# Two-level seven-product scheme for the first MLP layer of batches 2 and 3, with its left-hand sums made in batch 1 and the Fourier front woven into the second layer before it

## The chip, the core and the metric

The kernel runs on one core of a Trainium2 chip. The metric is the device time of one launch in microseconds, the median of several runs. All arithmetic that matters here is fp32.

## What is computed

Four batches go through bucketed (hash) attention. Its output is rearranged to `x` of 768 rows by 512 columns per batch and put through a Fourier mixing, a normalisation and a two-layer MLP:

```python
X = np.fft.fft(x, axis=1); X = np.fft.fft(X, axis=2)
u = x + np.real(X)
un = (u - mean(u)) / sqrt(var(u) + 1e-6)      # per row
out = u + np.maximum(un @ w_ch1, 0) @ w_ch2   # 512 -> 2048 -> 512
```

## The kernel before

**Stages.** Attention for all batches comes first, with an order written out by hand, and ends at about 337 us; what this text is about lies behind it. There each batch `b` goes through `mix(b)`: the Fourier front (`cs` matmuls L1071, `A` and `B` matmuls L1100, DVE adds L1114), then `mlp7(b)`: first layer and second layer. The output of the first layer is held transposed, features by rows of the sequence, in `hall`. Batch 0 also builds the weights' block sums; the times of the later batches are 508.5 to 674.8, 674.8 to 841.9 and 841.9 to 1012.8 us.

**First layer.** One level of the Strassen-Winograd scheme: a 2 by 2 block product with seven products instead of eight. The left blocks are pieces of `w_ch1` (names `A11, A12, A22` for the plain ones, `S1` to `S4` for sums), made once in batch 0 by `quarters` (L1184) and stored to the DRAM tensor `ad` (L1196, L1197), 128 KB each. From batch 1 on, a ring of 12 slots takes them back from `ad` (L1357, on the SP queue); the trace calls these loads `w<-ad`. The right blocks are halves of `x` and four sums of them. A `product` (L1373) is two matmul instructions of 128x128 by 128x384 (L1384). For one block row `f`, `inner` (L1409) makes seven products; some accumulate on each other in PSUM (`px` holds the running sum, `p2` and `p5` two others). ACT copies `px` and `p5` to `hall` (L1424, L1431, L1434), DVE adds a bank to it (L1427, L1437, L1440), ACT applies relu (L1398, L1447). Eight block rows in two halves of four give 56 products a batch.

**Second layer.** `outer7(half)` (L1253) follows each half: again one level of the scheme, 7 products per row tile `j` of 256 columns (L1279), with sums of `hall` on DVE (L1263 to L1265), DVE adds of the results (L1291) and ACT copies (L1305). Its right blocks `w<-bd` (7 of 512 KB, L1284) are fetched again on SP's queue at the end of each `outer7`. So a batch is `inner(0)`, `outer7(0)`, `inner(1)`, `outer7(1)`; in batch 1 they stand at about 530, 566, 602.4 and 638.5 us.

**What else runs beside.** `across` (L1121) turns `u` back by PE transposes into a bank `un` and copies it out on ACT (L1127). `fold(b + 1)` (DVE, L971 on) prepares the next batch's front, stepped in `outer7(0)`. `guard` (L1471) reads all of q and k again (384 KB a load on POOL's queue, `nq`, three buffers, L1481) and squares them on ACT (L1492); its result decides in batch 3 whether a fallback is taken. `store` (L939) writes the output on POOL's queue for batches 0 to 2.

**What sets the order.** Each engine, and each DMA queue with the engine that issues into it, works its instructions strictly in order. In this part a scheduler orders the instructions by need, except where `in_turn()` (L693) ties an instruction behind the last one that was noted in `done_by`. Generators are stepped beside each other: a function yields, and what is stepped at the yield gets its place there. `pt` hands out one of the eight PSUM banks.

Of the kernel before, what the change touches and what calls it, by code (L numbers as in the profile page):

```python
# [20 lines left out]
P = 128  # L21
# [462 lines left out]
def _main(  # L484
# [567 lines left out]
        for _ in scale(m, doos, dacc, dpk):  # L1052
            pass

    def mix(b):
        x = xs[b]
        z = zs[b]


        hd = DM // 2  # L1060
        F = late.tile([P, 2, 2, 2, DM], F32, tag="F", name=f"F{b}")
        nc.gpsimd.memset(F[:, :, 1, :, 0 : hd + 1 : hd], 0.0)
        for par in range(2):
            for t in range(NT // 2):
                ps = pt([P, DM], f"cs{b}_{par}_{t}")
                kinds = (0, 1) if t == 1 else (par ^ (t // 2),)
                for pc in range(2):
                    lo = 0 if 0 in kinds else hd // 2 + 1 - pc
                    hi = hd if 1 in kinds else hd // 2 + 1 - pc
                    for cp in range(2):  # L1070
                        nc.tensor.matmul(  # L1071
                            ps[:, pc + 2 * lo : pc + 2 * hi - 1 : 2],
                            z[:, cp, pc, par, t * P : (t + 1) * P],
                            ch[:, cp, pc, lo:hi], start=(cp == 0), stop=(cp == 1),
                        )
# [14 lines left out]
                yield  # L1090

        for j in range(NDC):
            pa, pb = (pt([P, HALF + 1], f"{nm}{b}_{j}") for nm in "AB")
            for par in range(2):
                cols = slice(par * NK, HALF + 1 if par else NK)
                for k, ps in enumerate((pa, pb)):
                    for t in range(2):
                        nc.tensor.matmul(  # L1100
                            ps[:, cols], F[:, par, k, t, j * P : (j + 1) * P],
                            sq[:, t, k, cols], start=(t == 0), stop=(t == 1),
                        )
# [13 lines left out]
            yield  # L1117

        yield from mlp7(b)

    def across(b, T, u):  # L1121

# [22 lines left out]
    with tc.manual_schedule(engines={ET.PE, ET.DVE, ET.Activation, ET.Pool, ET.SP}):  # L1145
# [18 lines left out]
        for i in range(NR)  # L1164
    ]
    at = NR * 2 * P
    bs = [
        w1f[:, at + i * S : at + (i + 1) * S].rearrange("p (k n) -> p k n", k=2)
        for i in range(3)
# [1 line left out]
    at += 3 * S  # L1171
    us = [w1f[:, at + i * DM : at + (i + 1) * DM] for i in range(4)]
    at += 4 * DM
    HD = DM // 2
    tq = late.tile([P, 8, HD], F32, tag="tq", name="tq")
    s2s = [
# [2 lines left out]
    ]  # L1179
    temps = [tq[:, i : i + 2] for i in (4, 6)]  # L1180

    qs = late.tile([P, 2, 4, HD], F32, tag="qs", name="qs")

    def quarters(f):  # L1184

# [30 lines left out]
    def weights2():  # L1216
# [14 lines left out]
        for half in range(2):  # L1231
# [18 lines left out]
            if half == 0:  # L1250
                yield

    def outer7(b, half, hall, ut, rs, s1s):  # L1253
        def tile_sums(j):
            if half == 0:
# [13 lines left out]
        for j in range(GT):  # L1269
# [18 lines left out]
            t6, t7 = (temps[j % 2][:, i] for i in range(2))  # L1288

            def add(t, r, cols, src):  # L1290
                nc.vector.scalar_tensor_tensor(  # L1291
                    t[:, cols], src, r, t[:, cols], op0=ALU.mult, op1=ALU.add
                )

# [10 lines left out]
            nc.scalar.copy(t6, px)  # L1305
# [5 lines left out]
            nc.scalar.copy(t7, px)  # L1311
            add(v, rv, high, t7)
            if half:
                store(b, j + GT, v, high)
# [14 lines left out]
    def mlp7(b):  # L1329
# [18 lines left out]
            ss = [s1s[0], spare[3].rearrange("p (r n) -> p r n", n=P)]  # L1348
        prods = [A11, A12, S2, S1, S3, S4, A22]
        right = {A11: b11, S2: t2, A12: b21, S1: t1, S3: t3, S4: b22, A22: t4}  # L1350
        todo = [(f, i) for f in range(HF) for i in prods]
        fetched = [0]

# [55 lines left out]
        def inner(half):  # L1409
            for r in range(HF // 2):  # L1410
# [41 lines left out]
                if r % 2:  # L1452
                    yield

        for half in range(2):
# [7 lines left out]
            ahead = fold(b + 1) if half == (b == 0) and b < B - 1 else iter(())  # L1463
            for _ in outer7(b, half, hall, ut, rs, ss):
                next(ahead, None)
                yield
            for _ in ahead:
                pass


    def guard():  # L1471

        nq = {}

        def fetch(i):
            if i < 2 * NPAIR * B:
                n, io = divmod(i, 2)
                b, t = divmod(n, NPAIR)
                tl = late.tile([P, S], F32, tag="nq", name=f"nq{i}", bufs=3)
                s = (k if io else q)[b, 2 * t : 2 * t + 2].rearrange("h s d -> (h s d)")  # L1480
                nc.gpsimd.dma_start(tl, s.rearrange("(p c) -> p c", p=P))  # L1481
                nq[i] = tl

        with in_turn():
            fetch(0)
            fetch(1)
        yield
        for i in range(2 * NPAIR * B):
            with in_turn():
                fetch(i + 2)  # L1490
                junk = late.tile([P, S], BF16, tag="junk", name=f"junk{i}")
                nc.scalar.activation(  # L1492
                    junk, nq.pop(i), AF.Square,
                    accum_out=norms[:, i % 2, i // 2 : i // 2 + 1],
                )
            yield

    def after(n, one, two):

        for i, _ in enumerate(one):  # L1500
            if i >= n and (i - n) % 2 == 0:
                next(two, None)
            yield
        for _ in two:
# [4 lines left out]
    for b in range(B):  # L1509
# [24 lines left out]
        if b == 1:  # L1534
            guards = guard()
        if 0 < b < B - 1:
            other = after(2, other, islice(guards, NPAIR * B + 1))
# [51 lines left out]
```

## Time and profile before

| what | value |
|---|---|
| median of 3 runs | 1013.13 us (1012.83 to 1014.03) |
| the profiled execution: its time | 1014.53 us |
| the profiled execution: its span | 1012.8 us |
| PE busy over the span | 1000.4 us (99%) |
| DVE, ACT, POOL busy | 623.2, 465.2, 86.3 us |
| granted TensorE clock | 0.999 |
| DMA, mean of the span | 114 GB/s |

"PE" is the matrix engine, "PEld" its weight loads, "DVE", "ACT" and "POOL" the vector, scalar and GpSimd engines, "SPq" and "POOLq" the DMA queues that SP and POOL issue into. Every fp32 matmul instruction leaves two records in the trace, so a product of two instructions is four records; where rows stand merged, "x4" is one product. "Idle before, releaser" is the time in which an engine had nothing to do ahead of an instruction, and what ended it.

### The profile page before, as it was taken

What the parts mean: (1) busy time and instruction counts of PE and PEld (TensorE: products, weight loads), DVE (VectorE), ACT (ScalarE), POOL (GpSimd) and SP (SyncE); (2) the same over time, 40 slices, a digit from 0 to 9 for tenths busy, and PEclk for the clock granted to TensorE, in tenths of its full rate; (3) what the DMA queues carried; (4) which work ended last, traced back from release to release, by engine and by line L of the source; (5) the groups of instructions that cost most, each with busy time, mean ns of one, the idle gap of its engine ahead of it and who ended that gap; (6) DMA issues with size and microseconds to landing.
All of it is one profiled execution on the core that took longest, in us unless ns stands there. A gap on an engine that the chain in (4) does not pass through costs nothing.

```text
span 1012.8 us, 14094 instructions
## 1 busy us (share of the span) xinstructions
PE 1000.4 (99%) x5169; PEld 650.7 (64%) x5169; DVE 623.2 (62%) x1086; ACT 465.2 (46%) x909; POOL 86.3 (9%) x179
## 2 busy tenths in 40 slices
PE   8999999999999999999999999999999999999997
PEld 5444444444444756866885785897586689678576
DVE  4788898878987597467869421529442344443142
ACT  5787877878766564065045413124512301420310
POOL 3000000000000112100213100122200020100000
PEclk9999999999999999999999999999999999999999
DMA  9545363554610447036445543164516323324301
GB/s 142 124 90 113 85 161 54 121 97 96 132 46 8 135 134 272 1 114 234 130 146 171 167 158 102 58 198 125 164 45 201 90 76 133 89 58 129 100 21 45
DMA packets 174877, 115.59 MB, mean 114 GB/s; under 512 B 126672, under 2 KB 159952, under 8 KB 174800
## 3 DMA queue, kind: packets, MB, share of 16 engines
q1 hardware_dynamic: 166224, 88.12, 32.4%
q0 software_dynamic: 7008, 26.09, 8.4%
q8 instruction: 43, 0.70, 0.3%
q10 hardware_dynamic: 1568, 0.39, 0.2%
q14 instruction: 34, 0.28, 0.1%
HBM read 93.59 MB, written 20.97 MB: 113 GB/s over the span
## 4 chain that ended last, share of the span: by engine, by line
PE 84%; issue 5%; DVE 5%; DMA 3%; POOL 1%; ACT 1%; SPq 0%; POOLq 0%; DVEq 0%; ACTq 0%
PE o L1279 27%; PE oo L875 13%; PE sc L858 12%; PE h_px L1384 11%; PE h_p L1384 8%; PE sc L848 4%; PE cs L1071 3%; PE A L1100 2%; PE B L1100 1%; PE sum L895 1%; PE bits L812 1%; DMA zraw<-in_moe_w_ch_dram 1%; DVE x L1114 1%; DVE bs L1132 1%; DMA kn<-in_k_dram 0%
## 5 line engine op out<-in xcount | busy, mean ns | idle before, releaser
L1279 PE MATMUL o<-w,h 128*128 128x256 f32 x960 | 212.6, 379 | 1.3 <-ACT tq L1305 1.3
L1279 PEld LDWEIGHTS o<-w,h 128*128 128x128 f32 x960 | 182.3, 190 | 28.1 <-ACT tq L1305 2.1
L865 ACT ACTIVATE pk<-sc 128x768 f32<-128x768 f32 x192 | 152.5, 813 | 34.9 <-PE sc L858 31.5
L858 PE MATMUL sc<-qt,kt 64*128 64x384 f32 x768 | 155.6, 482 | 0.0
L875 PE MATMUL oo<-pk,vn 128*64 128x385 f32 (+1 forms) x768 | 134.5, 492 | 0.0
L932 DVE TENSOR_TENSOR acc<-acc,pk 128x1536 f32<-128x1536 f32 x63 | 110.1, 1748 | 3.1
L875 PEld LDWEIGHTS oo<-pk,vn 128*64 128x64 f32 x768 | 50.9, 136 | 81.0 <-issue 79.2
L858 PEld LDWEIGHTS sc<-qt,kt 64*128 64x128 f32 x768 | 69.5, 188 | 30.5 <-issue 30.0
L1384 PE MATMUL h_px<-x,w 128*128 128x384 f32 x224 | 82.4, 489 | 0.0
L1305 ACT COPY tq<-o 128x256 f32<-128x256 f32 x24 | 8.9, 370 | 159.2 <-PE o L1279 159.2
L1384 PE MATMUL h_p<-x,w 128*128 128x384 f32 x224 | 81.7, 487 | 0.1
L1291 DVE SCALAR_TENSOR_TENSOR w<-o,rs,w 128x256 f32<-128x256 f32 x88 | 42.4, 482 | 61.3 <-PE o L1279 60.8
L1398 ACT ACTIVATE h<-h 128x384 f32<-128x384 f32 x72 | 37.7, 524 | 86.2 <-DVE h L1437 38.9
L1384 PE MATMUL h_px<-w 128*128 128x384 f32 x192 | 70.1, 488 | 0.0
L1384 PEld LDWEIGHTS h_p<-x,w 128*128 128x128 f32 x224 | 42.4, 190 | 29.5 <-DVE x L1114 0.7
L1384 PEld LDWEIGHTS h_px<-x,w 128*128 128x128 f32 x224 | 41.6, 190 | 28.3 <-ACT h L1431 2.7
L1437 DVE TENSOR_TENSOR h<-h,h_px 128x384 f32<-128x384 f32 x32 | 17.6, 550 | 65.1 <-PE h_px L1384 64.4
L1427 DVE TENSOR_TENSOR h<-h,h_p 128x384 f32<-128x384 f32 x32 | 17.6, 552 | 60.6 <-PE h_p L1384 60.4
L1384 PEld LDWEIGHTS h_px<-w 128*128 128x128 f32 x192 | 35.9, 190 | 25.7 <-DVE h L1437 1.6
L848 PEld LDWEIGHTS <-kk 33*128 33x128 bf16 x384 | 19.7, 93 | 50.9 <-issue 28.5
L1279 PE MATMUL o<-w,tq 128*128 128x256 f32 x192 | 45.5, 380 | 0.4 <-DVE w L1291 0.4
L1279 PE MATMUL o<-w 128*128 128x256 f32 x176 | 41.7, 379 | 0.0
(163 smaller groups left out, 1388.7 us busy)
## 6 DMA issues: line engine op xcount, KB each, us to landing
w<-ad SPq DMA_DIRECT2D x168, 128.0 KB, 2.1
w<-bd SPq DMA_DIRECT2D x42, 512.0 KB, 4.5
zraw<-in_moe_w_ch_dram SPq DMA_DIRECT2D x16, 512.0 KB, 4.5
zraw<-in_moe_w_ch_dram POOLq DMA_DIRECT2D x16, 512.0 KB, 4.0
bd<-w SPq DMA_DIRECT2D x14, 512.0 KB, 3.6
vn<-in_v_dram SPq DMA_DIRECT2D x32, 192.0 KB, 3.1
nq<-in_q_dram POOLq DMA_DIRECT2D x16, 384.0 KB, 3.9
nq<-in_k_dram POOLq DMA_DIRECT2D x16, 384.0 KB, 3.7
```

What stands on the lines that cost most here:

```text
L848: nc.tensor.matmul(pss[g][:, h, 0:HALF], kk[r, ks], bits[1][r] if g else bits[0][r, h], start=start, stop=not start,)
L858: nc.tensor.matmul(pss[g][:, h, 0:HALF], kt[rows, ks], qt[rows, g * HALF : (g + 1) * HALF], start=early, stop=not early,)
L865: nc.scalar.activation(pk[:, g, :, 0:HALF], pss[g][:, :, 0:HALF], AF.Exp, scale=SCALE)
L875: nc.tensor.matmul(oos[g][h * D : (h + 1) * D, 0:w], nat["v", n][:, (2 * c + h) * D : (2 * c + h + 1) * D], pk[:, g, h, 0:w], start=(c == ...
L932: nc.vector.tensor_tensor(acc, (first[:, :, :, 0:HALF] if c == 1 else acc), new, op=ALU.add)
L1071: nc.tensor.matmul(ps[:, pc + 2 * lo : pc + 2 * hi - 1 : 2], z[:, cp, pc, par, t * P : (t + 1) * P], ch[:, cp, pc, lo:hi], start=(cp == 0) ...
L1100: nc.tensor.matmul(ps[:, cols], F[:, par, k, t, j * P : (j + 1) * P], sq[:, t, k, cols], start=(t == 0), stop=(t == 1),)
L1279: nc.tensor.matmul(ps, a[:, r], right7[i][:, r], start=start and r == 0, stop=r == HF // 2 - 1, skip_group_check=not start,)
L1291: nc.vector.scalar_tensor_tensor(t[:, cols], src, r, t[:, cols], op0=ALU.mult, op1=ALU.add)
L1384: nc.tensor.matmul(ps, left[:, k], right[i][:, k], start=start and k == 0, stop=k == 1, skip_group_check=not start,)
L1398: done_by[ET.Activation] = nc.scalar.activation(h, h, AF.Relu)
L1427: done_by[ET.DVE] = nc.vector.tensor_tensor(c11, c11, p2, op=ALU.add)
```

## The change

Batches 0 and 1 keep their first layer, batches 2 and 3 (`b >= TWO`) get another one. Four parts:

1. **Two levels.** Each of the seven products of a half is done by the seven-product scheme again: over the four block rows of a half, 7 x 7 = 49 leaves, so 98 a batch; a leaf is two matmul instructions of 128x128 by 128x192. Inner running sums stay in PSUM (three banks `h..._0`, `_1`, `_2` for each outer product); `placed` takes them out, `behind` adds outer results up. Each left block is still 128 KB: 42 of the 98 are read from two block rows of `ad`, the others from a new DRAM tensor `ad2`.
2. **Mixing of the left blocks** (`blocks2`), once, in batch 1: 14 times a load of 512 KB from `ad` on SP's queue, four DVE sums of 128x256, a store of 512 KB to `ad2` on POOL's queue, in two slots. The seven of half 0 are stepped in `outer7(0)`, those of half 1 in `inner(1)`, where `fold(2)` is stepped too.
3. **The front** of batches 2 and 3, and the sums of the right blocks (`first_parts`), are stepped in `outer7(1)` of the batch before, instead of standing by themselves between the batches; all six `across` come ahead of the first leaf.
4. **`guard`** has one buffer instead of three; it fetches at one yield and squares two yields later, stepped at every yield.

```diff
+        if b >= TWO:
+            yield from first_parts(b)
...
+    HH = HALF // 2
+    S12, S22, S32, S42 = range(4)
+    LEAVES = ("a11", "a12", S22, S12, S32, S42, "a22")
+    TWO = 2
+    ad2 = tc.dram_tile([2, 7, 4, P, 2, P], F32, name="ad2")
+
+    def blocks2():
+        for half in range(2):
+            rows = slice(half * HF // 2, (half + 1) * HF // 2)
+            slots = late.tile([P, 2, 2, 8 * P], F32, tag="r2", name=f"blocks{half}")
+            def fetch(i):
+                if i < 7:
+                    src = slots[:, i % 2, 0].rearrange("p (f k m) -> p f k m", k=2, m=P)
+                    nc.sync.dma_start(src, ad[rows, i].rearrange("f p k m -> p f k m"))
+            fetch(0)
+            fetch(1)
+            yield
+            for i in range(7):
...
+                nc.vector.tensor_tensor(s1, lc, ld, op=ALU.add)
+                nc.vector.tensor_tensor(s2, s1, la, op=ALU.subtract)
+                nc.vector.tensor_tensor(s3, la, lc, op=ALU.subtract)
+                nc.vector.tensor_tensor(s4, lb, s2, op=ALU.subtract)
+                nc.gpsimd.dma_start(ad2[half, i].rearrange("s p g m -> p s g m"), dst)
+                fetch(i + 2)
+                yield
...
...
+                if b == TWO - 1 and half:
+                    step(beside)
+                    step(second)
                 yield
...
+            if half:
...
+                beside = fold(1) if b == 0 else front(b + 1) if b < B - 1 else iter(())
+            for i, _ in enumerate(outer7(b, half, hall, ut, rs, ss)):
...
+                elif half or b >= TWO:
+                    step(beside)
+                else:
+                    if i % 3 == 0:
+                        step(beside)
+                    if i % 2 == 0:
+                        step(second)
...
+    def two_levels(b, right, ut, ss):
...
+                    src = ad[f : f + 3 : 2, i, :, k].rearrange("g p m -> p g m")
+                else:
+                    src = ad2[half, i, j]
+                nc.sync.dma_start(ring[fetched[0] % NR], src)
...
+        for T in (0, 3, 1, 4, 2, 5):
+            across(b, T, ut[T])
+        last_parts(b)
...
+                at_bank = (0, 1, 0, 2, 0, 2, 0)[j]
...
+                for g in range(2):
+                    nc.tensor.matmul(
+                        ps[at_bank][:, g], ring[n % NR][:, g], parts[i][j],
+                        start=start and g == 0, stop=g == 1, skip_group_check=True,
+                    )
+                fetch()
+                placed(i, j, ps)
+                if j == 6:
+                    behind(i)
...
+            s = (k if io else q)[b, 2 * t : 2 * t + 2].rearrange("h s d -> (h s d)")
             with in_turn():
+                nc.gpsimd.dma_start(side, s.rearrange("(p c) -> p c", p=P))
+            yield
+            yield
+            with in_turn():
                 nc.scalar.activation(
+                    side, side, AF.Square,
```

How the order moves at three places. The lines of the new kernel are its own: the leaves' matmuls are L1716, the second layer's L1375, the block loads L1331, the block sums L1341 to L1344, the block stores L1345, the ring's loads L1456 (batch 1) and L1623 (batches 2 and 3), the loads of `bd` L1380, the first layer's adds of batches 0 and 1 L1526, L1536 and L1539, its matmuls there L1483.

First, DVE in the second half of batch 1's first layer. Before, the adds of `h_6` and `h_7` (block rows 6 and 7 of that layer) stand one behind the other; the sums for the second layer follow:

```order
L1427 TENSOR_TENSOR h_4117<-h_4117,h_6_p_4627 128x384
L1437 TENSOR_TENSOR h_4117<-h_4117,h_6_px 128x384
L1440 TENSOR_TENSOR h_4117<-h_4117,h_6_p_4636 128x384
L1427 TENSOR_TENSOR h_4117<-h_4117,h_7_p_4655 128x384
L1437 TENSOR_TENSOR h_4117<-h_4117,h_7_px 128x384
L1440 TENSOR_TENSOR h_4117<-h_4117,h_7_p_4663 128x384
L1263 TENSOR_TENSOR w_2989<-h_4117 128x512 x2
```

Now the four sums of the last left block (`blocks`) stand ahead of the first add of `h_7`:

```order
L1536 TENSOR_TENSOR h_4107<-h_4107,h_6_px 128x384
L1539 TENSOR_TENSOR h_4107<-h_4107,h_6_p_4685 128x384
L1341 TENSOR_TENSOR blocks_4542<-blocks_4542 128x256
L1343 TENSOR_TENSOR blocks_4542<-blocks_4542 128x256
L1342 TENSOR_TENSOR blocks_4542<-blocks_4542 128x256
L1344 TENSOR_TENSOR blocks_4542<-blocks_4542 128x256
L1526 TENSOR_TENSOR h_4107<-h_4107,h_7_p_4705 128x384
L1536 TENSOR_TENSOR h_4107<-h_4107,h_7_px 128x384
L1539 TENSOR_TENSOR h_4107<-h_4107,h_7_p_4714 128x384
L1359 TENSOR_TENSOR w_2989<-h_4107 128x512 x2
```

So the first add of `h_7`, and with it the bank that the add gives free, now comes behind sums that read a block that was loaded in this stage; 12 more blocks stand further ahead in the same way.

Second, SP's queue over batch 1. Before, the ring's loads of a half (28) and the 7 loads of `bd` take turns:

```order
L1284 DMA w_2989<-bd 128x1024
L1357 DMA w_134<-ad 128x256
L1284 DMA w_2989<-bd 128x1024 x6
L1357 DMA w_134<-ad 128x256 x28
L1284 DMA w_2989<-bd 128x1024 x7
```

Now the loads of blocks stand among them, those of half 0 ahead of the loads of `bd` at the end of `outer7(0)`, those of half 1 among the ring's loads of `inner(1)`:

```order
L1380 DMA w_2989<-bd 128x1024 x7
L1456 DMA w_134<-ad 128x256 x28
L1331 DMA blocks_4299<-ad 128x4x256 x4
L1380 DMA w_2989<-bd 128x1024 x2
L1331 DMA blocks_4299<-ad 128x4x256
L1380 DMA w_2989<-bd 128x1024 x5
L1456 DMA w_134<-ad 128x256 x4
L1331 DMA blocks_4542<-ad 128x4x256 x2
L1456 DMA w_134<-ad 128x256 x5
```

A block's load (from the third of each half on) waits for the DVE sums that read the slot before, and the rows behind it on SP wait with it. On POOL the 14 block stores stand among the loads of `guard`.

Third, PE at the end of the first half of batch 3's first layer. Before, all products of `h_3` are through before the second layer's first matmul:

```order
L1384 MATMUL h_3_px<-w_134 128x384 x2
L1384 MATMUL h_3_p_5996<-w_134 128x384 x2
L1384 MATMUL h_3_px<-x_2306,w_134 128x384 x2
L1384 MATMUL h_3_p_5996<-x_2306,w_134 128x384 x2
L1384 MATMUL h_3_px<-w_134 128x384 x2
L1279 MATMUL o_0_0_0_6032<-w_2989,h_5860 128x256 x4
L1279 MATMUL o_0_0_1_6038<-w_2989,h_5860 128x256 x4
```

Now the last leaves (`h_0_6` is the last outer product of half 0, the third number the bank) stand among the second layer's first matmuls, in the scheduler's order:

```order
L1716 MATMUL h_0_2_0_6293<-sums_6016,w_134 128x192 x2
L1716 MATMUL h_0_6_2_6361<-sums_6016,w_134 128x192
L1375 MATMUL o_0_0_0_6398<-w_2989,h_6140 128x256
L1716 MATMUL h_0_6_0_6330<-x_2306,w_134 128x192 x2
L1375 MATMUL o_0_0_0_6398<-w_2989,h_6140 128x256 x3
L1375 MATMUL o_0_0_1_6404<-w_2989,h_6140 128x256
L1716 MATMUL h_0_6_2_6361<-x_2306,w_134 128x192 x2
L1375 MATMUL o_0_0_1_6404<-w_2989,h_6140 128x256
L1716 MATMUL h_0_6_0_6330<-sums_6016,w_134 128x192 x2
L1375 MATMUL o_0_0_1_6404<-w_2989,h_6140 128x256 x2
L1375 MATMUL o_0_0_4_6417<-w_2989 128x256 x3
L1375 MATMUL o_0_0_0_6398<-w_2989,tq 128x256 x4
```

The matmuls of `o_0_0_4` (which read the sums in `w_2989`) and of `tq` come right behind the last leaf; at this place before, eight other matmuls of `o_0_0_0` and `o_0_0_1` stood between.

More of the change, by code (lines that the diff above doesn't have):

```diff
@@ L1166, in _main @@
     at = NR * 2 * P
+    AT = at
     bs = [
@@ L1453, in inner, with halves, step @@
                     yield
+        yield from halves(b, hall, ut, rs, ss, inner)
+    folds2 = {}
+    def halves(b, hall, ut, rs, ss, inner):
+        def step(gen):
+            with in_turn():
+                next(gen, None)
+        beside = iter(())
+        if 0 < b < B - 1:
+            beside = fold(b + 1)
+        if b == TWO - 1:
+            second = blocks2()
         for half in range(2):
@@ L1462, in mlp7 @@
                     across(b, T, ut[T])
-            ahead = fold(b + 1) if half == (b == 0) and b < B - 1 else iter(())
-            for _ in outer7(b, half, hall, ut, rs, ss):
-                next(ahead, None)
-                yield
-            for _ in ahead:
-                pass
-    def guard():
[L1473 to L1487, printed above, removed]
+            if half:
+                for _ in beside:
+                    pass
+                if b == TWO - 1:
+                    for _ in second:
+                        pass
+                beside = fold(1) if b == 0 else front(b + 1) if b < B - 1 else iter(())
@@ L1488, in guard @@
+    def guard():
         for i in range(2 * NPAIR * B):
+            n, io = divmod(i, 2)
+            b, t = divmod(n, NPAIR)
+            s = (k if io else q)[b, 2 * t : 2 * t + 2].rearrange("h s d -> (h s d)")
             with in_turn():
[L1490 to L1491 removed]
+                nc.gpsimd.dma_start(side, s.rearrange("(p c) -> p c", p=P))
+            yield
+            yield
+            with in_turn():
                 nc.scalar.activation(
[L1493 removed]
+                    side, side, AF.Square,
@@ L1496, in guard, with after @@
             yield
-    def after(n, one, two):
+    def after(n, one, two, every=2):
         for i, _ in enumerate(one):
-            if i >= n and (i - n) % 2 == 0:
+            if i >= n and (i - n) % every == 0:
                 next(two, None)
```

167 lines of the change are left out of this document (160 added, 7 removed).

## Prediction

> **What bounds the kernel now.** I read the page's span, engines and chain of waits first:
>
> ```profile
> span 1012.8 us, 14094 instructions
> PE 1000.4 (99%) x5169; PEld 650.7 (64%) x5169; DVE 623.2 (62%) x1086; ACT 465.2 (46%) x909; POOL 86.3 (9%) x179
> PE 84%; issue 5%; DVE 5%; DMA 3%; POOL 1%; ACT 1%; SPq 0%; POOLq 0%; DVEq 0%; ACTq 0%
> ```
>
> PE is busy for 99% of the span and carries 84% of the chain, so the kernel is bound by the matrix engine, and there is no slack on it: a matmul saved is time saved, and a new wait of PE is time lost. Next come windows over the places that the change touches: the second layer and the first layer of batch 1, then three stretches with much traffic. Columns: window, length, busy time and count of PE, PEld, DVE, ACT, POOL, the granted clock, the busy share of the DMA engines, GB/s.
>
> ```profile
> 566.00:602.40 36.40, 35.98 (x167) 31.39 (x166) 16.16 (x32) 8.04 (x21) 3.76 (x7) 1.00 0.49 152
> 602.40:638.50 36.10, 36.10 (x114) 21.28 (x113) 7.21 (x14) 13.48 (x27) 0.00 (x0) 1.00 0.41 125
> 592.00:607.00 15.00, 15.00 (x64) 11.88 (x63) 4.54 (x9) 2.22 (x5) 0.00 (x0) 1.00 0.80 261
> 785.00:805.00 20.00, 20.00 (x64) 11.79 (x63) 4.25 (x8) 7.83 (x16) 0.00 (x0) 1.00 0.33 99
> 392.00:402.00 10.00, 9.46 (x44) 6.87 (x43) 8.10 (x19) 3.60 (x9) 2.83 (x5) 1.00 0.95 354
> ```
>
> `outer7(0)` (first row) and `inner(1)` (second) leave PE no gap; DVE and ACT have over half their time free. The DMA engines are half used there: that share is what the mixing of the blocks will draw on.
>
> **The matmuls.** A row is start, duration, engine, line, operation; a duration reaches past the next start, since matmuls are pipelined, so I take differences of starts.
>
> ```profile
> 942.13 1.46 PE L1384 MATMUL h_px<-w 128*128 128x384 f32 x4
> 943.42 0.81 PE L1384 MATMUL h_px<-x,w 128*128 128x384 f32 x2
> 691.51 0.81 PE L1100 MATMUL B<-sq,F 128*128 128x192 f32 x4
> 692.16 1.04 PE L1126 MATMUL un<-ident,x 128*128 128x128 f32 x8
> ```
>
> A product of 384 columns takes 943.42 - 942.13 = 1.29 us (the 28 of the 36.10 us window: 1.29 each). A leaf has the shape of the Fourier front's matmuls, four records of 192 columns: 692.16 - 691.51 = 0.65 us. Per batch 56 x 1.29 = 72.2 us become 98 x 0.655 = 64.2 us: -8.0, for two batches -16.
>
> **New chains in batches 2 and 3.**
>
> ```profile
> 943.62 0.49 ACT L1447 ACTIVATE h<-h_px 128x384 f32<-128x384 f32 x1 [0.18 <-PE h_px L1384]
> 708.61 0.46 ACT L1431 COPY h<-h_px 128x384 f32<-128x384 f32 x1
> 709.12 1.56 PE L1384 MATMUL h_px<-x,w 128*128 128x384 f32 x4
> L1440 DVE TENSOR_TENSOR h<-h,h_p 128x384 f32<-128x384 f32 x32 | 17.7, 553 | 15.1 <-PE h_p L1384 15.1
> L1434 ACT COPY h<-h_p 128x384 f32<-128x384 f32 x32 | 15.2, 475 | 14.5 <-PE h_p L1384 14.1
> L1127 ACT COPY w<-un 128x512 f32<-128x512 f32 x16 | 8.7, 592 | 12.1 <-PE un L1126 11.9
> L1398 ACT ACTIVATE h<-h 128x384 f32<-128x384 f32 x72 | 37.7, 524 | 86.2 <-DVE h L1437 38.9 <-DVE h L1427 33.5 <-DVE h L1440 13.8
> L1263 DVE TENSOR_TENSOR w<-h 128x512 f32<-128x512 f32 x24 | 15.9, 685 | 3.7 <-ACT h L1398 3.5 <-ACT h L1407 0.2
> 868.60 1.31 PE un L1126 x12
> 638.54 36.26 PE o L1279 x168
> ```
>
> A bank that is read between two accumulations costs 943.62 - 943.42 = 0.20 from the product's end to ACT's start, 0.475 for the copy (DVE's add 0.55), and 709.12 - 708.61 - 0.46 = 0.05, taken as up to 0.16 with the pipeline's fill, until PE goes on: 0.84 to 0.91 us. Three other leaves, 3 x 0.655 = 1.97 us, usually stand between two on the same bank, so that is hidden. It shows in two places.
> - At a batch's start six `across` (24 transposes at 1.31 / 12 = 0.11, 2.6 us) hand ACT six copies of 0.59 one behind the other, and the first leaf's copy stands behind them: 4 x 0.11 + 0.20 + 6 x 0.59 = 4.2, and 0.475 + 0.16 more, 4.8 us; PE has 2.6 + 2 leaves = 3.9 us to do. Loss 0.9 a batch.
> - At a half's end the second layer's `o_..._4` reads sums made after the last add: 0.20 + 0.55 + 0.05 + 0.52 + 0.05 + 0.685 + 0.16 = 2.2 us (0.52 is the relu). The eight matmuls that covered it now stand in part among the last leaves; three are left, at 36.26 / 168 = 0.216 a record or 0.43 an instruction 1.3 us. Loss 0.9, and with two adds in halves 1.2; at the fourth end (batch 2's second half) the front's `cs` matmuls cover it: 3 x 1.2 = 3.6.
>
> Together 1.8 + 3.6 + some 0.6 for small ones: +6. Bounds: +2 if the scheduler's three matmuls and ACT's order do better, +9 if each end loses both.
>
> **The block mixing.** It draws on DMA engines, DVE, and two queues, all in `outer7(0)` and `inner(1)` of batch 1.
>
> ```profile
> L1194 DVE TENSOR_TENSOR qs<-w,qs 128x256 f32<-128x256 f32 x8 | 3.4, 419 | 0.0
> L714 POOL DMA_DIRECT2D zraw<-in_moe_w_ch_dram x16 | 8.6, 541 | 93.7 <-DVE qs L1192 33.4 <-ACT zraw L663 22.2 <-DVE w L1244 8.2
> w<-bd SPq DMA_DIRECT2D x7, 512.0 KB, 4.3
> w<-bd SPq DMA_DIRECT2D x7, 512.0 KB, 5.0
> ad<-qs SPq DMA_DIRECT2D x1, 512.0 KB, 5.9
> w<-ad SPq DMA_DIRECT2D x1, 128.0 KB, 4.5
> w<-ad SPq DMA_DIRECT2D x168, 128.0 KB, 2.1
> zraw<-in_moe_w_ch_dram POOLq DMA_DIRECT2D x1, 512.0 KB, 5.3
> ```
>
> The rows of transfers are count, size and us from issue to landing: `bd` from 591 to 607 us, `bd` from 664 to 682, three rows of the busy stretch at 392 to 402, and the ring's loads over the span. DVE: 14 x 4 sums x 0.42 = 23.5 us, in stages where it has 20 and 29 us free, so its time alone costs nothing. The bytes do. Those two stages now move 36.4 us x 152 + 36.1 x 125 GB/s = 10.0 MB. The mixing adds 14 loads and 14 stores of 0.524 MB; two loads are made earlier and the last store may come late, so 25 of them, 13.1 MB, must pass before DVE can make the last sums. These stand in DVE's order ahead of `h_7`'s first add, due when its second product ends: 36.4 + 23 x 1.29 + 0.2 = 66.3 us. So 23.1 MB in 66.3 us, 348 GB/s, without a pause. At full use of its engines the trace shows, by GB/s over busy share: 99 / 0.33 = 300 (the ring's loads, in pieces of 1 KB as the blocks'), 261 / 0.80 = 326 (`bd` in larger pieces) and 354 / 0.95 = 372 (a stage of larger transfers in both directions). That gives 77, 71 or 62 us. To it come about 6 us in which the mixing can't keep the engines busy (half 1's first load waits in the same buffer for half 0's last store, then lands: 0.54 + 5.9 + 5.3 = 11.7 us, with the other traffic at about half of the rate going on), and 4 x 0.42 = 1.7 us for the last sums. PE can run on past a late add until `h_7` wants the bank again, in its last product: (27 - 23) x 1.29 = 5.2 less 0.2 + 0.55 + 0.55 + 0.3 = 3.6 us. The stall is then 77 + 7.7 - 66.3 - 3.6 = 14.8 at 300 GB/s, 8.8 at 326, none at 372.
>
> A second way to it is the chain of slots. Half 0's last sums stand ahead of `h_4`'s first add (2 x 1.29 + 0.2 = 2.8 us into `inner(1)`). From there: issue 0.54, store 5.9, load 5.3 by the loaded landings above, so half 1's first sums are ready at 14.5 us. Two slots give two blocks each 1.7 + 0.54 + 5.9 = 8.1 us; the seventh comes at 14.5 + 3 x 8.1 = 38.8, plus 1.7 = 40.5, due at 29.9: 10.6 - 3.6 = 7 us of stall, even where bandwidth is enough. Behind such a late load stand the ring's loads on SP, behind the sums stand PE's adds on DVE. I take +12, between the first two rates and nearer the first, whose transfers have the blocks' piece size; bounds 0 (it only adds work) and +15.
>
> In batches 2 and 3 a leaf eats 128 KB in 0.655 us, 200 GB/s, where a product took 125 GB/s with all else. The ring's 12 slots then give 12 x 0.655 = 7.9 us of lead against a landing of 2.1, or 4.5 under load: 0. The `ad` leaves' pieces of 512 bytes have no row here; were they at half rate, 98 + 42 loads of 0.131 MB in 64 us would be 287 GB/s, still under 300, so the upper bound is +1.
>
> **The guard.**
>
> ```profile
> nq<-in_q_dram POOLq DMA_DIRECT2D x16, 384.0 KB, 3.9
> L1492 ACT ACTIVATE junk<-nq 128x768 bf16<-128x768 f32 x32 | 27.0, 843 | 6.2 <-DMA nq<-in_k_dram 3.7 <-DMA nq<-in_q_dram 2.4
> ```
>
> With one buffer the Square waits for a load issued two yields before. A yield of the first layer is some 2.6 us, so 5.2 against 0.54 + 3.9: hidden, until the load lands as late as the 5.0 to 5.9 above, or a yield is short. Then ACT waits with the copies of the first layer behind it, and those hold PE's banks; ACT already waits 6.2 us for these loads with three buffers. +2, bounds 0 and +4.
>
> **The front.** Its matmuls and adds are the same; woven into the second layer, the chain from `cs` to the DVE adds is covered by `o` matmuls. 168 records of `o` run through in 36.26 us today, and PE hardly waits in the front: -0.5, bounds -2 and 0. The sums of `first_parts` and `last_parts` are DVE work in its free half: nothing; without that cover they would delay the first leaves of `S4` and `A22`, which stand last.
>
> **Sum.** -16 + 6 + 12 + 2 - 0.5 = +3.5. The profiled execution took 1014.5 (span 1012.8 and 1.7 around it), the median is 1013.1; 1014.5 + 3.5 = 1018 on the one, 1016.6 on the other: 1017.
>
> **The rivals.**
> - *The transfers are absorbed*: faster. For it speaks 372 GB/s over ten microseconds, with loads and stores mixed as here. The mixing then costs 1, the guard 0.5: -16 + 6 + 1 + 0.5 - 0.5 = -9, so 1004 (999 to 1011). It decides from a rate of about 355 GB/s up. Against it: no stretch as long as 66 us comes near that, and the slot chain loses without regard to the rate.
> - *The overload spreads*: with 300 GB/s the chain is late too (7), ring loads queued on SP behind block loads hold PE through `inner(1)`, and `outer7(1)` starts on late `bd` loads. 15 + 7 + 3 for the guard: -16 + 6 + 25 - 0.5 = +14.5, so 1028 (1022 to 1035).
> - *The gain and the losses cancel* (326 GB/s, a stall of 8.8): -16 + 6 + 8.8 + 2 - 0.5 = 0, so 1013 (1011 to 1015).
> - *Leaves run slower than their columns*, held by weight loads: 196 instructions of two loads at the 189 ns below are 74 us, more than the 72.2 of today, so nothing is saved:
>
> ```profile
> L1100 PEld LDWEIGHTS B<-sq,F 128*128 128x128 f32 x128 | 21.6, 189 | 0.0
> ```
>
>   Against it: these loads belong to the front's matmuls of the same shape, and four records there run at 0.655 with a load each. Under 0.03, within the overload.
>
> [...]
>
> **How the numbers follow.** Forecast, the late transfers outweigh the matmuls (1015.1 to 1022): 0.40. Spread overload: 0.18. Cancelled: 0.12. Absorbed: 0.30. A measurement tells changes from about 0.2%, 2 us. So faster 0.30, same 0.12, slower 0.58. The likeliest case's own range is 1015 to 1022; the range that leaves no more than 2 in 10 out reaches from 1002 into the absorbed case to 1029 into the overload.
>
> **What the profile after would show.** Right: four records of L1716 at 0.65 us; gaps on PE in batch 1's `inner(1)`, ended by DVE adds or ring loads, while DVE waits at L1341 for block loads; block and ring loads landing well above 4.5 and 2.1 us; a DMA share near 1 over some 70 us; gaps of about a microsecond at `o` after three half-ends; ACT waiting at L1740 for loads. Wrong: batch 1 no longer than the 166 us of its row, or leaves over 0.70 us.
>
> ```profile
> 508.50:674.80 166.30, 165.88 (x699) 125.56 (x698) 82.33 (x162) 52.71 (x120) 24.45 (x45) 1.00 0.44 136
> ```
>
> What would make the prediction wrong most easily is the rate that the DMA engines hold when loads and stores overlap.

## The result and the profile after

The changed kernel takes 1025.09 us (median of 5 runs, 1020.7 to 1025.71), beside 1013.2 of the kernel before on the same chip: ratio 1.0105, 95% interval 1.0084 to 1.0127. It is 12 us slower. Its profiled execution, which the rows below come from, took 1025.1 with a span of 1023.3, so spans stand 10.5 apart. The page's span, engines and chain:

```profile
span 1023.3 us, 15369 instructions
PE 990.9 (97%) x5505; PEld 696.2 (68%) x5505; DVE 723.3 (71%) x1272; ACT 483.1 (47%) x933; POOL 92.2 (9%) x193
PE 79%; issue 9%; DVE 4%; DMA 3%; POOL 2%; ACT 1%; SPq 0%; POOLq 0%; DVEq 0%; ACTq 0%
```

PE has 9.5 us less to do (990.9 for 1000.4, and part of the 990.9 runs at a lower clock, below), yet the span is longer. Behind 500 us PE waited 1.3 us in all before; now its waits there, listed further down, come to 21.5. Before:

```profile
PE o L1279 <- ACT tq L1305: 1.3, 2, 0.8
```

From the timeline of PE, the first matmul of each stage in both profiles gives a table of where the 10.5 us are (us):

| stage | before | after | difference |
|---|---|---|---|
| up to `outer7(0)` of batch 1 | 565.3 | 564.3 | -1.0 |
| `outer7(0)` of batch 1 | 36.9 | 37.6 | +0.7 |
| `inner(1)` of batch 1 | 36.1 | 51.5 | +15.4 |
| `outer7(1)` of batch 1 and front of 2 | 53.8 | 53.7 | -0.1 |
| batch 2 from its `across` to that of batch 3 | 167.1 | 164.9 | -2.2 |
| batch 3 from there to the end | 153.6 | 151.2 | -2.3 |

One stage of 36 us loses 15.4; two batches gain 2.2 and 2.3 where the prediction's terms for them come to 5 each. The next rows are windows over `outer7(0)` and `inner(1)` of batch 1 (columns as before), then the waits of PE behind 500 us (for what, us in total, times, longest), then the chain's pieces of leaves.

```profile
564.30:601.90 37.60, 36.51 (x169) 31.84 (x168) 31.23 (x68) 7.94 (x20) 6.79 (x11) 1.00 0.69 228
601.90:653.50 51.60, 40.84 (x114) 22.43 (x113) 30.07 (x74) 16.04 (x35) 9.38 (x15) 0.93 0.91 317
603.00:612.00 9.00, 6.61 (x20) 3.58 (x19) 6.09 (x15) 2.68 (x6) 2.05 (x3) 0.94 1.02 408
```

```profile
PE h L1716 <- ACT h L1648: 5.6, 2, 3.0
PE h_px L1483 <- ACT h L1530: 5.3, 3, 2.5
PE o L1375 <- DVE w L1359: 3.7, 3, 1.3
PE h_px L1483 <- DVE h L1536: 3.1, 2, 1.8
PE h_p L1483 <- ACT h L1533: 2.7, 1, 2.7
PE o L1375 <- DVE u L1387: 1.1, 1, 1.1
```

```profile
714.31 31.74 PE h L1716 x176
...
786.70 29.29 PE h L1716 x180
```

- *Batch 1.* The waits at L1483, 5.3 (of which 0.3 stands in `inner(0)`), 3.1 and 2.7 us, are 10.8 us in `inner(1)`. There the DMA engines are busy for 0.91 of the time. The clock is granted at 0.93 in the mean, and 0.07 of 51.6 us is another 3.6 us lost; about 1 of the 15.4 us is left over.
- *Leaves.* 180 records, 45 leaves, in 29.29 us: 0.651 us each. But 176 records at the start of batch 2 take 31.74, 3.1 us more than at that rate.
- *Starts and ends.* 5.6 us at two starts of a two-level batch, 3.7 us at three half-ends. The remaining 1.1 us (L1387) stands in `outer7(0)` of batch 1.

Who held DVE and ACT in batch 1, and how late the transfers of `inner(1)` landed, show the waits of both engines between 560 and 655 us and the transfers between 603 and 650:

```profile
DVE blocks L1341 <- DMA ad<-blocks: 6.0, 4, 2.2
DVE blocks L1341 <- DMA blocks<-ad: 5.9, 4, 2.3
ACT w L1740 <- DMA w<-in_q_dram: 8.1, 3, 5.3
ACT w L1740 <- DMA w<-in_k_dram: 2.8, 2, 1.4
```

```profile
ad<-blocks POOLq DMA_DIRECT2D x9, 512.0 KB, 6.2
blocks<-ad SPq DMA_DIRECT2D x7, 512.0 KB, 6.0
w<-ad SPq DMA_DIRECT2D x25, 128.0 KB, 5.2
```

A ring load of 128 KB takes 5.2 us instead of 2.1. DVE waits for stores and loads of blocks, ACT for the guard's loads, and PE for both. Two of PE's five gaps show how, by start, duration and, in brackets, idle time before:

```profile
608.28 0.84 ACT L1740 ACTIVATE w<-w 128x768 f32<-128x768 f32 x1 [1.71 <-DMA w<-in_q_dram]
609.63 1.73 PE L1483 MATMUL h_px<-x,w 128*128 128x384 f32 x4 [2.39 <-ACT h L1530]
620.58 0.42 DVE L1341 TENSOR_TENSOR blocks<-blocks 128x256 f32<-128x256 f32 x1 [1.79 <-DMA blocks<-ad]
622.85 0.52 ACT L1497 ACTIVATE h<-h 128x384 f32<-128x384 f32 x1 [3.00 <-DVE h L1526]
624.61 2.93 PE L1483 MATMUL h_p<-x,w 128*128 128x384 f32 x4 [2.70 <-ACT h L1533]
```

The first ends at a copy behind a square that waited for a guard load. The second ends at a copy behind a relu that waited for a DVE add, which stood behind block sums that waited for block loads. (The chain of waits leads through POOL's issues here, since stores wait for sums and the guard's loads for squares; PE's own waits are the clearer view.)

The start of batch 2 shows another wait that the prediction had not. Rows of the timeline, ACT and PE:

```profile
711.70 0.58 ACT L1186 COPY w<-un 128x512 f32<-128x512 f32 x1 [1.82 <-DMA out_dram<-w]
713.29 0.58 ACT L1186 COPY u<-un 128x512 f32<-128x512 f32 x1 [1.01 <-DMA out_dram<-u]
713.77 0.48 ACT L1648 COPY h<-h 128x384 f32<-128x384 f32 x1
714.31 1.97 PE L1716 MATMUL h<-sums,w 128*128 128x192 f32 x5 [3.04 <-ACT h L1648]
```

The last two copies of `across` write buffers from which the stores of the batch before (`out_dram<-w`, `out_dram<-u`) are still reading: 1.82 + 1.01 us. The copy of the first leaf stands behind them, and PE waits 3.04 us for it. (At the start of batch 3 the second of these copies waits 0.75 us for such a store. The profile puts the 1.62 us of the first down to a DVE sum; the store from that buffer, issued at 871.53 with some 4.7 us to landing, ended within 0.2 us of it.) Before the change, the front (some 18 us) stood between these stores and `across`. And behind this gap the clock is halved, as windows of 2 us show:

```profile
718.00:720.00 2.00, 2.00 (x8) 2.00 (x8) 0.09 (x1) 0.48 (x1) 0.00 (x0) 0.50 0.28 92
722.00:724.00 2.00, 2.00 (x14) 2.00 (x13) 1.43 (x4) 1.49 (x4) 1.37 (x4) 1.00 0.73 219
```

8 records in 2 us at a granted 0.50, 14 at 1.00: these are the 3.1 us that the first leaves take too long.

### The profile page after: what moved, and what is told of

It is laid out like the page before. It is cut to its first block, busy times and chain, and to the rows that moved or that the text cites. A ratio compares the mean times of both kernels' runs of the same rounds, so it can differ in the third digit from the quotient of the medians.

```text
span 1023.3 us, 15369 instructions
## 1 busy us (share of the span) xinstructions
PE 990.9 (97%) x5505; PEld 696.2 (68%) x5505; DVE 723.3 (71%) x1272; ACT 483.1 (47%) x933; POOL 92.2 (9%) x193
## 3 DMA queue, kind: packets, MB, share of 16 engines
q1 hardware_dynamic: 196464, 106.48, 37.6%
## 4 chain that ended last, share of the span: by engine, by line
PE 79%; issue 9%; DVE 4%; DMA 3%; POOL 2%; ACT 1%; SPq 0%; POOLq 0%; DVEq 0%; ACTq 0%
PE o L1375 24%; PE oo L875 13%; PE h L1716 12%; PE sc L858 12%; PE sc L848 3%; PE h_px L1483 3%; PE cs L1071 3%; PE h_p L1483 2%; PE A L1100 2%; PE B L1100 2%; DMA zraw<-in_moe_w_ch_dram 1%; PE sum L895 1%; PE bits L812 1%; POOL ad L1345 1%; DMA out_dram<-u 1%
## 5 line engine op out<-in xcount | busy, mean ns | idle before, releaser
L1375 PE MATMUL o<-w,h 128*128 128x256 f32 x960 | 217.2, 379 | 1.1 <-DVE u L1387 1.1
L1375 PEld LDWEIGHTS o<-w,h 128*128 128x128 f32 x960 | 180.8, 190 | 25.7 <-DVE u L1387 1.5
L1387 DVE SCALAR_TENSOR_TENSOR w<-o,rs,w 128x256 f32<-128x256 f32 x88 | 42.2, 480 | 54.3 <-PE o L1375 53.7
L1401 ACT COPY tq<-o 128x256 f32<-128x256 f32 x24 | 8.9, 372 | 146.6 <-PE o L1375 146.6
L1716 PE MATMUL h<-sums,w 128*128 128x192 f32 x336 | 61.7, 332 | 5.6 <-ACT h L1648 5.6
L1716 PEld LDWEIGHTS h<-sums,w 128*128 128x128 f32 x336 | 56.4, 193 | 6.9 <-ACT h L1648 6.4
L1716 PE MATMUL h<-x,w 128*128 128x192 f32 x256 | 52.5, 330 | 0.0
L1375 PE MATMUL o<-w 128*128 128x256 f32 x176 | 42.8, 380 | 3.7 <-DVE w L1359 3.7
L1375 PE MATMUL o<-w,tq 128*128 128x256 f32 x192 | 45.6, 380 | 0.4 <-DVE w L1387 0.4
L1716 PEld LDWEIGHTS h<-x,w 128*128 128x128 f32 x256 | 43.5, 192 | 1.4 <-DVE h L1654 0.8
L1407 ACT COPY tq<-o 128x256 f32<-128x256 f32 x24 | 8.9, 372 | 71.1 <-PE o L1375 71.1
L1483 PE MATMUL h_px<-x,w 128*128 128x384 f32 x96 | 36.2, 494 | 5.3 <-ACT h L1530 5.3
L1654 DVE TENSOR_TENSOR h<-h,h 128x384 f32<-128x384 f32 x52 | 28.6, 550 | 17.1 <-PE h L1716 12.7
L1375 PEld LDWEIGHTS o<-w,tq 128*128 128x128 f32 x192 | 36.2, 190 | 6.2 <-DVE w L1387 0.8
L1483 PE MATMUL h_p<-x,w 128*128 128x384 f32 x96 | 37.7, 518 | 2.7 <-ACT h L1533 2.7
```

The lines of the kernel that those rows point to most:

```text
L1375: nc.tensor.matmul(ps, a[:, r], right7[i][:, r], start=start and r == 0, stop=r == HF // 2 - 1, skip_group_check=not start,)
L1387: done_by[ET.DVE] = nc.vector.scalar_tensor_tensor(t[:, cols], src, r, t[:, cols], op0=ALU.mult, op1=ALU.add)
L1483: nc.tensor.matmul(ps, left[:, k], right[i][:, k], start=start and k == 0, stop=k == 1, skip_group_check=not start,)
L1654: done_by[ET.DVE] = nc.vector.tensor_tensor(d, x, y, op=ALU.add)
L1716: nc.tensor.matmul(ps[at_bank][:, g], ring[n % NR][:, g], parts[i][j], start=start and g == 0, stop=g == 1, skip_group_check=True,)
```

## The experiments

Each is the changed kernel with the edit shown; "before" on the chip of the first four is 1013.38 us, on that of the last four 1014.0. Ratios are to before, with their 95% intervals; "less" compares medians with the 1025.09 of the changed kernel. Its own runs lie up to 5 us apart, so differences of about 2 us are not told from nothing; the three values of before lie within 1 us.

**1. The guard's loads at an eighth of the bytes.**

```diff
-                nc.gpsimd.dma_start(side, s.rearrange("(p c) -> p c", p=P))
+                nc.gpsimd.dma_start(side[0:16], s.rearrange("(p c) -> p c", p=P)[0:16])
```

> The loads of the guard carry 16 of 128 partitions (48 KB instead of 384), all else as in the changed kernel; the squares work on what then stands in the buffer. Theory 'single buffer': of the five PE gaps in batch 1's inner(1) (10.8 us together) the two of 2.39 and 2.54 us end at ACT copies that stand behind a square whose load landed late; they go, with the half clock behind one of them, so inner(1) falls from 51.5 us to about 45.5 and the time by 6, to about 1019. Rival 'block bytes': the late block loads hold DVE and PE, the guard's waits only fill the same time; the 1.6 MB less of 15.4 in inner(1) bring 2 us at most, about 1023.

Measured 1018.7 us, ratio 1.0058 (1.0041 to 1.0075): 6.4 less. Windows of `outer7(0)` and `inner(1)`:

```profile
563.90:600.30 36.40, 36.40 (x169) 31.80 (x168) 31.12 (x68) 7.70 (x19) 6.91 (x11) 1.00 0.58 198
600.30:646.70 46.40, 39.23 (x114) 21.65 (x114) 29.98 (x74) 16.09 (x35) 9.09 (x14) 0.96 0.90 309
```

`inner(1)` is 46.4 us long, near the 45.5 of the first theory, though the DMA engines are as full as in the changed kernel (0.90). But it is not settled that the single buffer is the reason. Of the two gaps that the theory named, the 2.39 is gone and the 2.54 is 1.32, while the 2.70 grew to 3.51. The loads of 48 KB land in 4.5 to 5.4 us, hardly sooner than those of 384 KB (5.2 to 5.3), and the stage moves 14.3 MB instead of 16.4 (46.4 us x 309 GB/s, 51.6 x 317). So the guard's loads, by their lateness and by their bytes together, cost about 6 of the 16 us in batch 1; the run doesn't part the two.

**2. Block loads and stores at an eighth of the bytes.**

```diff
-                    nc.sync.dma_start(src, ad[rows, i].rearrange("f p k m -> p f k m"))
+                    w = P if i < 2 else 16
+                    nc.sync.dma_start(
+                        src[0:w], ad[rows, i].rearrange("f p k m -> p f k m")[0:w]
+                    )
...
-                nc.gpsimd.dma_start(ad2[half, i].rearrange("s p g m -> p s g m"), dst)
+                nc.gpsimd.dma_start(
+                    ad2[half, i].rearrange("s p g m -> p s g m")[0:16], dst[0:16]
+                )
...
-                    src = ad2[half, i, j]
+                    src = ad[half * HF // 2 + j, i]
```

> Block loads (all but the first two of a half) and all block stores carry 16 of 128 partitions, 64 KB instead of 512; their number, order, DVE sums and waits stay; the leaves that read the mixed blocks read plain blocks of the same size instead. Theory 'bytes': inner(1) of batch 1 falls from 51.5 us to 37 to 38, outer7(0) to 37, the time by 14 to 15, to about 1010.5. Rival 'order' (the block sums ahead of the adds on DVE, the loads ahead of the ring's on SP, the single guard buffer): inner(1) stays above 45 us and the time above 1019.

Measured 1010.77 us, ratio 0.9976 (0.9967 to 0.9986): 14.3 less. (The kernel leaves out most of the mixing, so its output is another one.)

```profile
600.30:640.40 40.10, 37.09 (x113) 20.95 (x112) 29.68 (x74) 16.14 (x35) 7.00 (x14) 1.00 0.70 215
```

`inner(1)` falls to 40.1 us with all sums, waits and orders still there. What they cost without the bytes is at most 4.0 us against 36.1. Two gaps are left: 1.10 us behind a square that waited 1.02 us for its load, and 1.78 us behind a square and a relu that waited 2.08 us for DVE, which worked block sums first. The blocks' bytes are the main cause; they also make the guard's loads late, which land in 3.6 to 3.8 us here, and the gains of runs 1 and 2 together, 20.7, are more than the 16.1 that batch 1 lost. The small transfers also land sooner (2.1 us a block load, 2.4 a store, instead of 6.0 and 6.2), so the run doesn't tell full DMA engines from a chain of slots that waits for landings; run 6 takes that up for the loads.

**3. Copies of row tiles 2 and 5 behind the first leaves.**

```diff
-        for T in (0, 3, 1, 4, 2, 5):
+        for T in (0, 3, 1, 4):
             across(b, T, ut[T])
+        held = []
+        for T in (2, 5):
+            ps = pt([P, NDC, P], f"un{b}_{T}")
+            for c in range(NDC):
+                nc.tensor.transpose(ps[:, c, :], xs[b][:, c, T * P : (T + 1) * P], ident)
+            held.append((ut[T], ps))
...
                 placed(i, j, ps)
+                if n in (7, 9):
+                    u_, un_ = held.pop(0)
+                    with in_turn():
+                        copy(u_, un_.rearrange("p c n -> p (c n)"))
```

> In batches 2 and 3 the transposes of across stay ahead of the leaves, but ACT's copies of row tiles 2 and 5 come behind the copies of the first leaves. Theory 'output stores': these two copies waited for the stores of the batch before to free their buffers (1.82 and 1.01 us at batch 2), and the first leaf's copy stood behind them; the PE gaps of 3.04 and 2.57 us go, and with the first the stretch of 6 to 7 us at half clock behind it (3.2 us): -8 to -9, about 1017. Rival 'six copies in a row', the cause named in the prediction: the stores only move the wait to the next copy; -2 to -3, and half clock stays if a gap of 2 us or more is left.

Measured 1015.38 us, ratio 1.0025 (1.0014 to 1.0035): 9.7 less. The profiled execution was the longest of ten, 1020.2, with 55.0 us in batch 1's `inner(1)`, so only its waits behind 660 us are used. Those of PE are down to one row, the half-ends:

```profile
PE o L1375 <- DVE w L1359: 3.7, 3, 1.3
```

Both gaps at the starts are gone, and with them the half clock (granted 1.00 in all windows of 2 us from 713 to 721): 5.6 + 3.1 = 8.7 of the 9.7 us. Four copies in a row are still there, and no wait comes from them. That alone doesn't refute "six copies in a row": by the prediction's own sum four take 4.8 - 2 x 0.59 = 3.6 us, less than PE's 3.9. It is the rows at the start of batch 2, 1.82 + 1.01 us of waiting for stores, that tell the two apart.

**4. The block steps spread over three stages.**

```diff
+                if b == TWO - 1 and not half and i % 3 == 0:
+                    step(second)
                 if b == TWO - 1 and half:
                     step(beside)
-                    step(second)
+                    if i % 2 == 0:
+                        step(second)
...
-                    if i % 2 == 0:
+                    if i % 3 == 1:
                         step(second)
```

> The 14 block steps are spread over inner(0), outer7(0) and inner(1) of batch 1 instead of the last two. Theory 'bytes': 30.5 MB in some 108 us are 282 GB/s, under what the DMA engines moved in inner(1) at full share (about 360): inner(1) falls from 51.5 to about 40, the time by 10 to 11, to about 1015. Rival 'order': the same block sums and guard squares stand in the same engines' orders, only elsewhere; gaps of the same size come up in inner(0), the time falls by less than 4.

Measured 1012.2 us (1009.71 to 1015.9), ratio 0.9994 (0.9977 to 1.0010): 12.9 less, about the time of before. Batch 1's three stages take 11.7 us of it. The three windows, `inner(0)` on:

```profile
534.90:564.90 30.00, 28.94 (x91) 16.58 (x90) 14.16 (x35) 13.82 (x31) 9.00 (x18) 1.00 0.72 237
564.90:601.10 36.20, 36.20 (x169) 31.87 (x168) 28.86 (x63) 7.78 (x19) 6.31 (x10) 1.00 0.67 220
601.10:641.40 40.30, 37.20 (x114) 20.92 (x113) 27.05 (x66) 16.30 (x35) 7.52 (x11) 1.00 0.96 338
```

`inner(1)` is 40.3 us long, as expected under "bytes". Its DMA engines are still full (0.96), and block loads, stores and ring loads land as late as before the edit (7.4, 6.1 and 5.2 us); but 13.6 MB pass in it (40.3 x 338) instead of 16.4. So late landings alone don't hold PE for long; what the run took out of the stage is bytes, and with them block steps. `inner(0)` is 30.0 us long instead of 29.0 in the changed kernel, with a new gap of 0.71, so "order" is not quite nothing.

**5. Runs 3 and 4 together.**

> The late copies and the early block steps together. Theory 'two separate losses' (transfers crowded into two stages of batch 1; copies behind output stores at the starts of batches 2 and 3): the gains of 9.7 and 12.9 us against 1025.1 add up, about 1002.5, faster than before by 1%. Rival 'one loss is the other's shadow' (the half clock behind a gap was counted in both, or the batches only start with other stores in flight): less than 18 us together, 1007 or more.

Measured 1004.85 us, ratio 0.9915 (0.9901 to 0.9930): 20.2 less than the changed kernel, where the sum would have been 22.6. The difference is within the spread of the runs, and the rival's "less than 18" is not met: two separate losses, nearly additive.

**6. Three buffers for block loads.** The buffer `r2` grows by 4 KB per partition for it.

```diff
-            slots = late.tile([P, 2, 2, 8 * P], F32, tag="r2", name=f"blocks{half}")
+            slots = late.tile([P, 5, 8 * P], F32, tag="r2", name=f"blocks{half}")
...
-                fetch(i + 2)
+                fetch(i + 3)
```

> The changed kernel with three buffers for block loads instead of two (two for the sums as before), so each load may start one block earlier; bytes, stages and the places of the sums stay. Theory 'bytes': in inner(1) the DMA engines were busy for 0.91 of the time, so loads that start earlier land as late; within 2.5 us of 1025.1. Rival 'chain of slots', the prediction's second way: DVE's 5.9 us of waiting for block loads in batch 1 go, and the adds behind them come earlier: -4 to -6, about 1020.

Measured 1023.18 us (1022.11 to 1024.53), ratio 1.0098 (1.0082 to 1.0113): 1.9 less, which is not clear of the noise (the changed kernel's interval is 1.0084 to 1.0127). DVE's waits at the blocks and `inner(1)`:

```profile
DVE blocks L1341 <- DMA ad<-blocks: 7.0, 5, 3.0
DVE blocks L1341 <- DMA blocks<-ad: 1.3, 2, 1.0
```

```profile
601.40:652.40 51.00, 42.35 (x114) 23.21 (x113) 30.02 (x74) 16.03 (x35) 9.11 (x14) 0.90 0.90 312
```

The waits for loads fall from 5.9 to 1.3 us, those for stores rise from 6.0 to 7.0, and the stage stays at 51.0 us with its engines as full as in the changed kernel. PE's gaps in it do fall, from 10.8 to 8.6 us, but more of it ran at half clock (0.90 granted in the mean, not 0.93; behind the last gap, of 2.35 us, four records took 2.72 us instead of 1.29). So the load slots are worth about 2 us at most. The prediction's chain counts the landing of a store in each slot, and these waits stayed: a third buffer for the stores was not tried, and that part stays open.

**7. Run 5 with a second guard buffer**, each load one item ahead.

```diff
...
+        fetch(0)
+        yield
         for i in range(2 * NPAIR * B):
...
+            fetch(i + 1)
             yield
             yield
             with in_turn():
                 nc.scalar.activation(
-                    side, side, AF.Square,
+                    sides[i % 2], sides[i % 2], AF.Square,
...
```

> Both as before, and a second buffer for the guard, each load issued one item ahead of its square. Theory: with the blocks spread, PE still waited 0.35, 0.71, 0.63 and 0.84 us in batch 1 for ACT copies that stand behind squares; these go, some -2 from the kernel with both edits. Rival: the loads land in time once the traffic is spread, and those gaps come from the late adds alone: no difference over 0.7 us.

Measured 1001.5 us, ratio 0.9879 (0.9864 to 0.9894), the fastest kernel of the study: 3.4 less than run 5. All waits of PE behind 500 us:

```profile
PE o L1375 <- DVE w L1359: 3.7, 3, 1.3
PE h_px L1483 <- DVE h L1536: 1.8, 1, 1.8
PE h_px L1483 <- ACT h L1530: 0.3, 1, 0.3
```

The waits behind squares are gone but for 0.3 us; run 5 still had 3.1 us at L1530.

**8. Run 7 with row tile 2 first in the second layer of batches 2 and 3.**

```diff
+        tiles = (2, 0, 1) if b >= TWO else (0, 1, 2)
...
-        for j in range(GT):
+        for n, j in enumerate(tiles):
```

with the late copies for tiles 1 and 4 in batch 3, since these are what batch 2 now stores last.

> As the one with two guard buffers, and in batches 2 and 3 the second layer takes its row tile 2 first, then 0 and 1; tile 2 lies in those columns of the first layer that the last leaf doesn't write. Theory 'half-end chain': the sums that o's third product reads can start two leaves earlier, and the three gaps of 1.16, 1.27 and 1.27 us at the half-ends go: -3 to -3.7. Rival: the leaf before the last (its add, its relu) binds as much, or the next tile's sums come late: -1 or less.

Measured 1003.87 us (999.92 to 1004.13), ratio 0.9888 (0.9870 to 0.9906), not clear of run 7. In batch 3 both half-end gaps shrank from 1.27 to 0.2 us, as the first theory has it; batch 2's is 1.36. But batch 3 takes 148.7 us as in run 7 (148.6). The end of the chain and the issues of the last stores, run 7 and then run 8:

```profile
994.22 0.48 DVE u L1387
994.73 0.33 SPq L947 DMA_DIRECT2D out_dram<-u  x1
```

```profile
994.54 0.49 DVE u L1390
993.32 2.35 SPq L947 DMA_DIRECT2D out_dram<-w  x2
995.77 1.18 SPq L947 DMA_DIRECT2D out_dram<-u  x2
```

From the start of this last add to the end of the span it takes 5.8 us in run 7 (span 1000.0) and 7.5 in run 8 (1002.0). The tile that now comes last, 1, is the one whose rows `store` writes in two pieces: SP was still issuing the two of the store ahead, and the last two came out by 996.95 instead of 995.06. So the gap was real, but its gain went into the tail.

## Why the prediction was right, and where it was not

It forecast slower, 1017 us in 1002 to 1029; measured were 1025, outside the 1015 to 1022 of its likeliest case. The mechanism it named, transfers of the mixing that outweigh the saved matmuls, is what runs 2 and 4 show. The time itself falls into the rival "the overload spreads" (1022 to 1035), though from other terms. Of the 8 us that are missing, 6.4 are the new chains with the clock behind them. Step by step:

- *Matmuls, -16.* Right: a leaf takes 0.651 us for the 0.655 taken from the front's rows, 98 of them 63.8 us against 72.2, -8.4 a batch. "Held by weight loads" is refuted.
- *New chains, +6.* The half-ends are right to a tenth, 3.7 us for 3.6, and stand where it put them. The starts are the step that failed: "six copies of 0.59 one behind the other" was put at 0.9 a batch; measured are 3.0 and 2.6 us, and 3.1 more at half clock. What the step left out is who else holds the buffers that the copies write. Moving the front out from between the batches took away the time in which the stores before were finished (some 18 us, where such a store landed in 4.6 to 5.2 us). The term is 12.4 instead of 6 (5.6 + 3.1 + 3.7).
- *Block mixing, +12, and guard, +2.* Together 14 against 16.1 in `outer7(0)` and `inner(1)`. That the sum is so near is luck, since two parts of it were wrong in opposite ways. The rate "300 GB/s at full use" was too low: over the whole of `inner(1)` GB/s over busy share is 317 / 0.91 = 348, and the engines moved 408 over nine microseconds. With 348 alone the prediction's own sum would have left a stall of 4.2 us. But "about 6 us in which the mixing can't keep the engines busy" was too small: they were busy for 0.69 of 37.6 us and 0.91 of 51.6, which is 16 us of pauses, where it had named a share near 1 over some 70 us. With both put right its sum gives 66.4 + 16.3 + 1.7 - 66.3 - 3.6 = 14.5 (an estimate). Seen by stage, `outer7(0)` moved only 37.6 x 228 = 8.6 MB, and 51.6 x 317 = 16.4 MB were left for the second stage; at 348 GB/s these need 47 us, in a stage of 36. The guard cost about 6 with its bytes (run 1) rather than 2. "Chain of slots, 7 us" is not borne out for the loads (run 6) and open for the stores.
- *The clock* has no term in it. 3.6 us in `inner(1)` (0.93 granted in the mean, 0.50 in the window from 612 to 614) and 3.1 at the start of batch 2 (0.50 from 718 to 720), 6.7 of the 10.5 us between the spans, are matmuls at half clock; they are counted in the terms above.
- *Front, -0.5.* 53.7 us against 53.8: nothing, as PE had hardly waited there before.
- *The rate in `inner(1)`* was no single figure: 408 GB/s over nine microseconds, at a busy share of 1.02, and 353 over 17, at 0.98:

```profile
603.00:620.00 17.00, 14.61 (x41) 8.14 (x40) 9.61 (x21) 5.18 (x11) 2.05 (x3) 0.90 0.98 353
```

## What to carry to other kernels

A mixing step that is done once is not free because its engines have time: count its bytes against the stage in which they must pass, and start it a stage earlier before buying buffers for it (12.9 us here for a few conditions in a loop; a third load buffer brought nothing clear of the noise). When work is moved out from between two stages, look for what it covered: here 18 us of front had hidden the stores that hold the next stage's buffers, and splitting a transpose from its copy was worth 9.7 us. With these two and a second guard buffer the same scheme goes from 1.0105 to 0.9879 of the time before.

## What the hardware showed that was not expected

A gap of PE cost more than its length where matmuls at half clock followed it. After a gap of 2.39 us in batch 1, matmuls ran at a granted 0.50; after one of 2.57 us at the start of batch 3, at 1.00.

```profile
609.63 1.73 PE L1483 MATMUL h_px<-x,w 128*128 128x384 f32 x4 [2.39 <-ACT h L1530]
612.00:614.00 2.00, 2.00 (x5) 1.09 (x4) 0.06 (x2) 0.52 (x1) 0.00 (x0) 0.50 1.00 369
878.73 1.57 PE L1716 MATMUL h<-sums,w 128*128 128x192 f32 x8 [2.57 <-ACT h L1648]
880.00:882.00 2.00, 2.00 (x14) 2.00 (x14) 1.24 (x5) 1.12 (x3) 0.79 (x2) 1.00 0.39 118
```

Run 2 shows it the other way round: behind a gap of 3.25 us at the start of batch 2 a leaf's four records took 0.65 us (702.88 to 703.53), and behind one of 2.19 us at the start of batch 3 they took 1.28 (864.53 to 865.81), about twice as long. So the length alone does not decide, and over its five runs the changed kernel's mean clock went from 0.990 to 0.995. What does decide, no run here shows. In the changed kernel the mean clock was 0.992 against 0.999 before.
